# Loading wq whole from one queue instead of in partition halves from two, in a decode-attention kernel

## The chip, the cores and the metric

The kernel runs on one core of one Trainium2 chip. The metric is the device time of one execution in microseconds (us), the median of several runs. Beside it stands one profiled execution, from which all durations come. Its span runs from the first to the last instruction of the program.

## The reference, cut to what matters

One token is decoded: x is one row of 512 values, in bf16.

```
A_x [1,1,512], A_wq [512,4096], A_wo [4096,512], k_cache, v_cache [1,8,65536,128]
q  = layernorm(x) @ wq                       # 32 heads of 128; 4 query heads share one KV head
p  = softmax(q . k / sqrt(128)) over 65536 keys
o  = p @ v                                   # per head
h  = x + o @ wo
h2 = h + (sigmoid(n @ w_gate) * (n @ w_up)) @ w_down,   n = layernorm(h)
```

The K and V caches are 8 heads x 65536 x 128 in bf16 each, together 268 MB; wq is 4 MB. All of it is read once.

## The kernel before, in words

**Data and buffers.** One big SBUF buffer, `ring`, holds 32 chunks of 16 x 128 elements in each of the 128 partitions; `CH` is one chunk (4 KB a partition). The K and V caches of a head come in three loads each, of 12, 8 and 12 chunks (`PIECES`), that is 6, 4 and 6 MB; the helper `load` (lines 318 to 324) issues them. Each load has 128 rows, one for each partition, so a 6 MB load is 128 pieces of 48 KB. wq lies in chunks 24 to 31 of `ring` (32 KB a partition: partition p holds rows 4p to 4p+3 of wq). The third K load of head 0, `K0.2`, goes to chunks 20 to 31, over wq, so it must wait until the q product has read wq.

**Who issues what.** `Prog` keeps one list of operations for each engine, written out by hand in order; `emit` turns them into programs with semaphore waits. All big loads are issued by SyncE (SP) from one queue, q1 in the profile, in this order: wq, K0.0, K0.1, K0.2 (waits for the q product, named `q`), K1.0 (waits for the first 12 chunks of K0 to be transposed, mark `F0.1`), V0.0 (mark `F0.3`), V0.1, K1.1 and so on, two heads interleaved. ScalarE (ACT) issues two small transfers from its own queue, q10.

**The start.** `emit` (lines 195 to 203) takes the first DMA of SP and of ACT out of their lists and puts each into the entry block ahead of the barrier (a Drain) with which every engine starts. The wq load is three DMAs (lines 326 to 328): chunks 0 and 1 of wq (8 KB a partition) for partitions 0 to 63 from SP, the same for partitions 64 to 127 from ACT, and chunks 2 to 7 (24 KB a partition) for all partitions from SP. All three count on one semaphore, `r0`. After the barrier ACT issues x (line 329: `x_col`, 128 pieces of 8 bytes, semaphore `x`).

**From x to K0.2.** VectorE (DVE) copies `x_col` (line 403), makes the layernorm with TensorE (PE, line 388) and GpSimd (POOL, line 399), and writes `xz` (line 406). PE then multiplies `xz` with wq: 32 matmuls in `project_q` (recorded on line 417) and a closing one (line 455). The end of that is `q`. ACT copies the result (line 459), DVE transposes it (line 462), ACT spreads it (line 464), and DVE begins the chunk transposes of K (line 498), 32 for each head in 128x1024 pieces. DVE runs its list in order: the transpose on line 462 stands before the first one on line 498. PE's scores, the softmax and the V product follow, and at the end the output projection and the MLP.

Of the kernel before, what the change touches and what calls it, by code (L numbers as in the profile page):

```python
# [35 lines left out]
class Prog:  # L36
# [14 lines left out]
    def op(self, eng, fn, deps=(), name=None, to=None, times=1):  # L51
        assert name is None or name not in self.where, name
        self.ops[eng].append(dict(fn=fn, deps=[d for d in deps if d], name=name, dma=None, to=to, times=times, part=self.part.get(eng)))
        if name:
            self.where[name] = (eng, len(self.ops[eng]) - 1)

    def dma(self, eng, fn, sem, deps=(), name=None):
        self.op(eng, fn, deps, name)
        rec = self.dma_sems.setdefault(sem, dict(sem=None, count=0))
        rec["count"] += 16  # L60
        self.ops[eng][-1]["dma"] = (sem, rec["count"])

    def emit(self):
# [24 lines left out]
        for e, ops in self.ops.items():  # L88
            n = 0
            for o in ops:  # L90
                if o["dma"]:
                    k, v = o["dma"]
                    value[o["name"]] = (self.dma_sems[k]["sem"], v, k)
                elif o["to"]:
                    k = o["to"]
# [24 lines left out]
        def put(e, eng, o, waits):  # L120
            for sem, v in waits:
                eng.wait_ge(sem, v)
            ins = o["fn"](eng)
            if o["dma"]:
                ins.then_inc(self.dma_sems[o["dma"][0]]["sem"], 16)
            elif o["to"]:
                ins.then_inc(extra[o["to"]], 1)
            elif o.get("inc"):
                ins.then_inc(sems[e], 1)
# [62 lines left out]
            self.nc.switch_bb(end)  # L192

        nc, entry = self.nc, self.nc.cur_bb.bb
        for e, eng, kind in (("sp", nc.sync, mybir.EngineType.SP), ("act", nc.scalar, mybir.EngineType.Activation)):
            first = self.ops[e].pop(0)
            assert first["dma"] and not first["deps"]
            put(e, eng, first, [])
            code = list(entry.instructions)
            load = code.pop()  # L200
            at = [i for i, ins in enumerate(code) if isinstance(ins, mybir.InstDrain) and ins.engine == kind]
            code.insert(at[0], load)
            entry.instructions = code
        entry = nc.cur_bb

        for e, eng in (("sp", nc.sync), ("pool", nc.gpsimd), ("act", nc.scalar), ("dve", nc.vector), ("pe", nc.tensor)):
# [10 lines left out]
def bass_sequential_preLN__gqa_block_cached__glu_gated_glu__decode_kernel(  # L217
# [10 lines left out]
    CH = TC * DH  # L228
    PIECES = ((0, 12), (12, 20), (20, 32))
    RING = 32 * CH  # L230
    AT = {"K": (0, 0, 8), "V": (12, 24, 20), "K0": (0, 12, 20), "V7": (0, 12, 20), "wq": 24, "wg": 0, "wd": 7}
# [7 lines left out]
    with ExitStack() as es:  # L239
        def sb(name, shape, dt):  # L240
            return es.enter_context(nc.sbuf_tensor(name, shape, dt))
# [14 lines left out]
        ring = sb("ring", [128, RING], bf16)  # L256
# [9 lines left out]
        x_col = sb("x_col", [128, 4], bf16)  # L266
# [41 lines left out]
        op, dma = P.op, P.dma  # L308


        W_SPLIT = {"wg": [(0, 4)], "wu": [(0, 3), (3, 4)]}
        W_AT = {"wg": AT["wg"] * CH, "wu": AT["wg"] * CH + 4 * FF}
        LAST = [(20, 28), (28, 32)]
# [9 lines left out]
            at = (first_chunk(k, h, q) - j0) * CH  # L323
            dma("sp", lambda e: e.dma_start(ring[:, at + a * CH:at + z * CH], rows[:, (a - j0) * CH:(z - j0) * CH]), sem, deps, name)  # L324

        for i, (eng, p0, p1, c0, c1) in enumerate((("sp", 0, 64, 0, 2), ("act", 64, 128, 0, 2), ("sp", 0, 128, 2, 8))):
            dst, rows = ring[p0:p1, (AT["wq"] + c0) * CH:(AT["wq"] + c1) * CH], A_wq.rearrange("(p k) n -> p (k n)", p=128)[p0:p1, c0 * CH:c1 * CH]
            dma(eng, lambda e, dst=dst, rows=rows: e.dma_start(dst, rows), "r0", (), "wq" if i == 2 else f"wq{i}")
        dma("act", lambda e: e.dma_start(x_col[:, :], A_x[0].rearrange("o (p k) -> (o p) k", k=4)), "x", name="x")
        for q in range(3):  # L330
            load("K", 0, q, ["q"] if q == 2 else (), f"r{q + 1}", f"K0.{q}")
        for h in range(1, HKV):
# [8 lines left out]
        for i, (j0, nj) in enumerate(WO):  # L341
            src = A_wo[j0 * DH:(j0 + nj) * DH, :].rearrange("(p r) n -> p (r n)", r=nj)
            dst = ktw[:, j0 * D:(j0 + nj) * D]
# [4 lines left out]
        for k, w in (("wg", B_w_gate), ("wu", B_w_up)):  # L348
            src = w.rearrange("(p k) n -> p (k n)", p=128)
            for i, (k0, k1) in enumerate(W_SPLIT[k]):  # L350
                at = W_AT[k]
# [3 lines left out]
        for i, (r0, r1) in enumerate(WD_SPLIT):  # L355
            at = AT["wd"] * CH
# [443 lines left out]
        for i, (nm, bank) in enumerate((("wg", GB), ("wu", UB))):  # L800
            at = W_AT[nm]
            for kt in range(4):
                for c in range(4):
                    dep = [f"{nm}.{j}" for j, (k0, _) in enumerate(W_SPLIT[nm]) if k0 == kt and c == 0]
                    op("pe", lambda e, at=at, kt=kt, c=c, bank=bank: e.matmul(  # L805
# [58 lines left out]
```

## Time and profile before

| | |
|---|---|
| time, median of 3 runs | 660.18 us (660.09 to 660.22) |
| profiled execution, its own time | 660.18 us |
| its span | 658.8 us |
| PE busy | 429.7 us, 65% of the span |
| DVE busy | 350.5 us, 53% |
| ACT busy | 42.9 us, 7% |
| bytes read by DMA | 282.33 MB, 429 GB/s over the span |
| queue q1 (SP) | 8434 packets, 281.81 MB, 99.2% of 16 DMA engines |
| queue q10 (ACT) | 224 packets, 0.53 MB, 0.4% |

The profile gives busy time and idle time of each engine, the chain of waits that ended last, and DMA issues with their time to landing. A DMA is cut into packets, one for each row, that 16 DMA engines move; the trace also holds a record of each packet (start, duration, bytes, queue). "Landing" is when the semaphore of a DMA is complete.

### The profile page before, as it was taken

The numbers are of one execution on the slowest core, as the hardware profiler recorded it, in microseconds if no ns is written. First come the engines' busy times: TensorE is split into PE (matmuls) and PEld (weight loads), VectorE is DVE, ScalarE is ACT, GpSimd is POOL, SyncE is SP. The second block draws the span as 40 slices with busy tenths as digits, with TensorE's granted clock in tenths as the row PEclk, the third lists the DMA queues.
The fourth block names the chain that finished last, engine by engine and source line by source line (L and its number), as shares of the span: only waits on it lengthen the run. The fifth ranks groups of instructions, "written<-read, shape, count | busy, mean of one in ns | idle before, by whom it ended". The sixth has DMA issues, their size and how long they took to land.

```text
span 658.8 us, 6242 instructions
## 1 busy us (share of the span) xinstructions
PE 429.7 (65%) x2315; PEld 69.0 (10%) x1547; DVE 350.5 (53%) x432; ACT 42.9 (7%) x114; POOL 3.6 (1%) x17
## 2 busy tenths in 40 slices
PE   0698576747568467675586476684766855765756
PEld 0100010011001010010000100010100101001212
DVE  2299845838167554647258290684636573573102
ACT  1100200020000200002000200002000020002001
POOL 1000000000000000000000000000000000000000
PEclk9988798777878587796786778785868967778855
DMA  9999999999999999999999999999999999999998
GB/s 350 414 459 433 414 436 424 442 445 419 446 430 430 430 430 462 430 430 430 422 449 436 442 417 430 430 433 442 431 446 430 430 430 430 459 433 410 440 422 336
DMA packets 8658, 282.34 MB, mean 429 GB/s; under 512 B 1105, under 2 KB 1106, under 8 KB 1618
## 3 DMA queue, kind: packets, MB, share of 16 engines
q1 hardware_dynamic: 8434, 281.81, 99.2%
q10 hardware_dynamic: 224, 0.53, 0.4%
HBM read 282.33 MB, written 0.00 MB: 429 GB/s over the span
## 4 chain that ended last, share of the span: by engine, by line
DMA 65%; PE 20%; DVE 11%; issue 3%; ACT 1%; SPq 0%; PEldq 0%; POOL 0%
DMA ring<-in_A_k_cache_dram 34%; DMA ring<-in_A_v_cache_dram 29%; PE PS L417 18%; DVE ktw L498 10%; DMA x_col<-in_A_x_dram 2%; PE PS L805 0%; ACT P_sb L544 0%; DVE M_sb L505 0%; PE PS L823 0%; PE PS L388 0%; PEldq L171 0%; DVE hh L815 0%; SPq L324 0%; SPq L344 0%; PE PS L619 0%
## 5 line engine op out<-in xcount | busy, mean ns | idle before, releaser
L498 DVE STREAM_TRANSPOSE ktw<-ring 128x1024 f32<-128x1024 f32 x256 | 292.5, 1210 | 170.5 <-DMA ring<-in_A_k_cache_dram 170.5
L417 PE MATMUL PS<-ktw 128*128 128x512 bf16 x1024 | 292.4, 437 | 116.6 <-DVE ktw L498 108.3
L417 PE MATMUL PS<-ring,PT_sb 128*32 x1024 | 99.6, 492 | 69.8 <-PEq L171 44.8
L417 PEld LDWEIGHTS PS<-ktw 128*128 x256 | 27.1, 106 | 371.6 <-issue 260.4
L587 ACT ACTIVATE po_sb<-PS,rl 128x512 bf16<-128x512 f32 x8 | 5.5, 687 | 522.7 <-PE PS L417 522.7
L417 PEld LDWEIGHTS PS<-ring,PT_sb 128*32 x1024 | 20.7, 116 | 145.6 <-issue 144.1
L505 DVE TENSOR_REDUCE M_sb<-PS 128x1 f32<-128x512 f32 x32 | 19.9, 684 | 20.5 <-PE PS L417 20.5
L533 DVE TENSOR_REDUCE gmj<-PS 1x4 f32<-1x128 f32 x8 | 2.2, 279 | 39.9 <-PE PS L531 39.9
L544 ACT ACTIVATE P_sb<-PS,negmax 128x512 bf16<-128x512 f32 x32 | 21.6, 686 | 0.3
L554 DVE STREAM_TRANSPOSE PT_sb<-P_sb 128x512 bf16<-128x512 bf16 x32 | 20.1, 682 | 1.7 <-ACT P_sb L544 1.7
L603 DVE TENSOR_TENSOR Lw<-O,blk_of 128x896 bf16<-128x896 bf16 (+1 forms) x2 | 1.4, 682 | 21.8 <-ACT O L593 21.8
L417 PE MATMUL PS<-ring,xz 128*8 x32 | 9.2, 459 | 2.3 <-DVE xz L406 2.3
L388 PE MATMUL PS<-st,onesf 128*128 128x2 f32 x4 | 1.2, 363 | 13.8 <-DVE st L387 13.8
L531 PE MATMUL PS<-identf,gm 128*1 128x128 f32 x16 | 4.5, 379 | 5.6 <-issue 3.4
L538 PE MATMUL PS<-one_f,gmrep 1*128 1x1 f32 x16 | 4.4, 345 | 5.0 <-DVE gmrep L535 5.0
L561 DVE TENSOR_REDUCE lsum<-PS 128x1 f32<-128x4 f32 x8 | 1.3, 162 | 11.8 <-PE PS L559 11.8
L544 ACT ACTIVATION_READ_ACCUMULATOR P_sb<-PS,negmax 128x1 f32 x32 | 6.5, 202 | 0.0
L462 DVE STREAM_TRANSPOSE qt<-qh 32x512 bf16<-32x512 bf16 x1 | 0.7, 699 | 10.7 <-ACT qh L459 10.7
L590 PE MATMUL PS<-sel_bf,po_sb 128*128 128x4 bf16 x32 | 2.1, 170 | 6.3 <-ACT po_sb L587 6.3
L417 PE MATMUL PS<-ktw,O 128*1 x26 | 5.8, 379 | 0.0
L559 PE MATMUL PS<-L_sb,lsel 128*128 128x4 f32 x16 | 2.5, 229 | 3.8 <-DVE PT_sb L554 3.8
L540 ACT ACTIVATE negmax<-PS 128x1 f32<-128x1 f32 x8 | 1.4, 171 | 55.4 <-PE PS L538 55.4
(82 smaller groups left out, 69.1 us busy)
## 6 DMA issues: line engine op xcount, KB each, us to landing
ring<-in_A_k_cache_dram SPq DMA_DIRECT2D x16, 6144.0 KB, 26.1
ring<-in_A_v_cache_dram SPq DMA_DIRECT2D x15, 6144.0 KB, 25.7
ring<-in_A_v_cache_dram SPq DMA_DIRECT2D x9, 4096.0 KB, 30.5
ring<-in_A_k_cache_dram SPq DMA_DIRECT2D x8, 4096.0 KB, 24.7
ktw<-in_A_wo_dram SPq DMA_DIRECT2D x1, 3584.0 KB, 14.7
ring<-in_A_wq_dram SPq DMA_DIRECT2D x1, 3072.0 KB, 13.3
ring<-in_A_v_cache_dram SPq DMA_DIRECT2D x1, 2048.0 KB, 38.4
ring<-in_B_w_gate_dram SPq DMA_DIRECT2D x1, 1792.0 KB, 30.7
```

The costliest lines, as they stand in the source:

```text
L417: return e.add_instruction(mybir.InstMatmult(name=nc.get_next_instruction_name(), engine=mybir.EngineType.PE, ins=[rhs, lhsT], outs=[e.low ...
L498: op("dve", lambda e, d=dst, sr=src: e.transpose(d, sr), deps, f"T{b}.{c}", to="T")
L505: op("dve", lambda e, u=u: e.tensor_reduce(M_sb[:, u % 4:u % 4 + 1], ps(u % NS, 0, 512), AX.X, ALU.max), [f"S{b}.{NC - NR + k}"], f"mx{u}" ...
L531: op("pe", lambda e: e.matmul(ps(MISC, 0, 128, 0, 1), lhsT=gm[:, :], rhs=identf[:, :], start=True, stop=True), [f"gm{h}"], f"gmT{h}", to="Q")
L533: op("dve", lambda e: e.tensor_reduce(gmj[:, :], ps(MISC, 0, 128, 0, 1).rearrange("p (i a c) -> p a i c", a=4, c=NC), AX.XY, ALU.max), [f" ...
L538: op("pe", lambda e: e.matmul(ps(MISC, 128, 129), lhsT=gmrep[0:1, :], rhs=one_f[0:1, 0:1], start=True, stop=True), [f"gmrep{h}"], f"neg{h}")
L540: op("act", lambda e: e.activation(negmax[:, k:k + 1], ps(MISC, 128, 129), AF.Copy, scale=-att_scale), [f"neg{h}"], f"negmax{h}")
L544: op("act", lambda e, b=b: e.activation(P_sb[:, (b % 4) * 512:(b % 4 + 1) * 512], ps(b % NS, 0, 512), AF.Exp, bias=negmax[:, k:k + 1], sca ...
L554: op("dve", lambda e, b=b: e.transpose(PT_sb[:, (b % 4) * 512:(b % 4 + 1) * 512], P_sb[:, (b % 4) * 512:(b % 4 + 1) * 512]), [f"E{b}"], f" ...
L559: op("pe", lambda e: e.matmul(ps(MISC, 132, 136), lhsT=lsel[:, :], rhs=L_sb[:, :], start=True, stop=True), [f"PT{NR * h + NR - 1}"], f"l{h ...
L587: op("act", lambda e: e.activation(po_sb[:, :], ps(PO, 0, 512), AF.Copy, scale=rl[:, :]), [f"PV{h}.{NR - 1}", f"rl{h}"], f"po{h}", to="po")
L590: op("pe", lambda e, t=t: e.matmul(ps(OX, 0, 4), lhsT=po_sb[:, t * 128:(t + 1) * 128], rhs=sel_bf[:, 8 * t:8 * t + 8:2], start=(t == 0), s ...
```

## The change

wq is loaded by one DMA from SP: all 128 partitions, 32 KB each, 4 MB. The two half loads and the 24 KB load are gone. `emit` puts only SP's first DMA ahead of the barrier; ACT's list now begins with x, which is issued after the barrier as before. Semaphore `r0` counts 16 instead of 48. Nothing else differs.

```diff
-        for e, eng, kind in (("sp", nc.sync, mybir.EngineType.SP), ("act", nc.scalar, mybir.EngineType.Activation)):
-            first = self.ops[e].pop(0)
-            assert first["dma"] and not first["deps"]
-            put(e, eng, first, [])
-            code = list(entry.instructions)
-            load = code.pop()
-            at = [i for i, ins in enumerate(code) if isinstance(ins, mybir.InstDrain) and ins.engine == kind]
-            code.insert(at[0], load)
-            entry.instructions = code
+        first = self.ops["sp"].pop(0)
+        assert first["dma"] and not first["deps"]
+        put("sp", nc.sync, first, [])
+        code = list(entry.instructions)
+        load = code.pop()
+        at = [i for i, ins in enumerate(code) if isinstance(ins, mybir.InstDrain) and ins.engine == mybir.EngineType.SP]
+        code.insert(at[0], load)
+        entry.instructions = code
...
+        dma("act", lambda e: e.dma_start(x_col[:, :], A_x[0].rearrange("o (p k) -> (o p) k", k=4)), "x", name="x")
...
-        for i, (eng, p0, p1, c0, c1) in enumerate((("sp", 0, 64, 0, 2), ("act", 64, 128, 0, 2), ("sp", 0, 128, 2, 8))):
-            dst, rows = ring[p0:p1, (AT["wq"] + c0) * CH:(AT["wq"] + c1) * CH], A_wq.rearrange("(p k) n -> p (k n)", p=128)[p0:p1, c0 * CH:c1 * CH]
-            dma(eng, lambda e, dst=dst, rows=rows: e.dma_start(dst, rows), "r0", (), "wq" if i == 2 else f"wq{i}")
-        dma("act", lambda e: e.dma_start(x_col[:, :], A_x[0].rearrange("o (p k) -> (o p) k", k=4)), "x", name="x")
+        dma("sp", lambda e: e.dma_start(ring[:, AT["wq"] * CH:(AT["wq"] + 8) * CH].rearrange("p (k n) -> p k n", k=4),
+                                        A_wq.rearrange("(p k) n -> p k n", p=128)), "r0", (), "wq")
```

## The prediction

> **What bounds the kernel now.** I read the page first, then the DMA issues, the SyncE queue's waits, the timeline and chain of the first 60 us, and last the packet records. The page says that the DMA engines are the bound:
>
> ```profile
> DMA  9999999999999999999999999999999999999998
> GB/s 350 414 459 433 414 436 424 442 445 419 446 430 430 430 430 462 430 430 430 422 449 436 442 417 430 430 433 442 431 446 430 430 430 430 459 433 410 440 422 336
> ...
> q1 hardware_dynamic: 8434, 281.81, 99.2%
> ```
>
> Only the first and the last slice move clearly less. The packet records agree: from 2.2 to 655.5 us at least 14 of 16 DMA engines are always at work, with never a gap on q1. So a microsecond saved in q1's stream at the start comes off the end, and a microsecond in which q1 runs dry is added, whatever PE and DVE do. Two things count: how fast wq passes, and whether the next load is issued before the queue is empty. The edit touches these rows:
>
> ```profile
> ring<-in_A_wq_dram SPq DMA_DIRECT2D x1, 3072.0 KB, 13.3
> ...
> ring<-in_A_wq_dram SPq DMA_DIRECT2D x1, 512.0 KB, 5.4
> ring<-in_A_wq_dram ACTq DMA_DIRECT2D x1, 512.0 KB, 7.5
> ...
> x_col<-in_A_x_dram ACTq DMA_DIRECT2D x1, 1.0 KB, 11.0
> ```
>
> 1 KB of x takes 11.0 us to land, and the chain of waits goes through it:
>
> ```profile
> 1.51 11.04 DMA x_col<-in_A_x_dram
> ...
> 16.09 9.21 PE PS L417 x32
> 25.30 0.23 PE PS L455
> 25.53 0.02 issue
> 25.55 27.90 DMA ring<-in_A_k_cache_dram
> ```
>
> x is read at 12.57, q is ready at 25.55, 12.98 us later, and SyncE then issues K0.2 in that moment. Today this costs nothing, since q1 still holds K0.0 and K0.1: K0.2's first packets come at 37.9 to 38.6 us (mean 38.24), directly behind K0.1's last. Between issue and first packet of a DMA with nothing ahead of it there are 1.37 us (the first wq load, 0.00 to 1.37) or 0.79 us (the output, 657.59 to 658.38); I take 1.1. So q has 38.2 - 1.1 - 25.55 = 11.6 us to spare, and x as much. That is the cover on which the change leans.
>
> **The change, part by part.**
>
> *wq in one load.* The halves run slowly. Alone, an 8 KB packet takes 0.31 us (w_down's, later); the 128 packets of the two halves average 0.54 (SP's) and 0.60 (ACT's): 8 per DMA engine, 2.15 + 2.39 = 4.54 us. The 24 KB packets take 0.912 us each once alone, 0.972 on the mean, since the first overlap ACT's half: 8 per engine, 7.78 us. Together 12.32 us. The windows show the two regimes:
>
> ```profile
> 1.40:6.90 5.50, 0.00 (x0) 0.00 (x0) 2.87 (x9) 1.87 (x2) 2.27 (x11) 1.00 1.06 253
> 7.40:13.70 6.30, 0.52 (x2) 0.50 (x2) 0.52 (x4) 0.00 (x0) 0.00 (x0) 1.00 1.01 433
> ```
>
> The last column is GB/s, 253 against 433. One load of 128 rows of 32 KB is shaped like K0.1, whose packets take 1.213 us without exception: 8 x 1.213 = 9.70. The very first packets of an execution are slow on their own account (0.8 where 0.31 is usual): 0.5 stays. So 12.32 - 10.2 = 2.1 us are gained. The bounds: 2.6 if the first packets aren't slow with full rows, nothing if the slow start is a warm-up that has nothing to do with halves (against it: many second and third packets, at 2.2 to 2.8 us, took 0.31 to 0.45, and the slowness came after). That 128 rows are queued instead of 64 may start some DMA engines later (the 64 rows' first packets spread over 1.4 to 2.2 us): 0 to 0.5. I take 2.1. Two DMAs fewer save 32 semaphore packets of 9 ns over 16 engines, nothing.
>
> *x comes to stand elsewhere in the order.* ACT issues x after the barrier at 1.5 us as before, but now as its first DMA, with wq (9.7 us of work) already in q1 and K0.0 (8 x 1.815 = 14.5 us) issued by SP at the same 1.50. Which goes first? The packet records show how the two queues share an engine:
> - wq0 (SP, 0.00) and wq1 (ACT, 0.12): on all 16 engines the four packets of wq0 and its semaphore come before the first of wq1, without alternation. The two issues ended 85 ns apart.
> - wq2 (SP, 1.504, ending 1.895) and x (ACT, 1.506, ending 1.863): on 15 engines all of x passes first, between 5.63 and 6.92 us. On one, three x packets pass and then one x per wq2 packet, at 7.51, 8.42, 9.34, 10.25, 11.17, and the semaphore at 12.09. That engine alone makes x land at 12.55 and not at 7.4.
>
> So an engine takes packets in the order in which the two queues' DMAs reached it, and mixes them one to one only where both arrive together; 30 ns decide. The first DMA on a queue takes longer to issue:
>
> ```profile
> L328 SPq DMA_DIRECT2D ring<-in_A_wq_dram x2: 391/483/575, 0.0 to 1.5; - x2
> L328 ACTq DMA_DIRECT2D ring<-in_A_wq_dram x1: 539/539/539, 0.1 to 0.1; - x1
> L329 ACTq DMA_DIRECT2D x_col<-in_A_x_dram x1: 357/357/357, 1.5 to 1.5; - x1
> ```
>
> 575 then 391 on SP, 539 then 357 on ACT. As ACT's first, x should take 539: it ends at 2.045. K0.0 as SP's second ends at 1.504 + 0.39 to 0.42 = 1.90 to 1.92. x is 0.13 us behind K0.0 where it was 0.03 ahead of wq2, and 0.3 ahead of K0.1 (from 1.945). It falls behind K0.0 on every engine. K0.0's last packets end at 28.9 - 2.1 = 26.8; x follows within 0.1 and, with the 0.48 us between its last packet and DVE's read today, is read at 27.4 instead of 12.57: 14.8 later. The bounds are 12.5 (x clean ahead of K0.0) and 37 (behind K0.1 too); I take 27.4, by the issue rows.
>
> *The wait that grows.* q then comes at 27.4 + 13.0 = 40.4, and K0.2's first packet at 41.5. K0.1's last ends at 38.2 - 2.1 = 36.1. q1 is dry for 5.4 us. Behind the waiting K0.2 in SP's list stand K1.0 and all others. K1.0 waits for 12 transposes on DVE, which start after line 462, now at 41.0 and done at 41.7 (29.34 before): with the 13.74 us that they take today (29.34 to 43.08) K1.0 is issued at 55.4, first packet 56.5. K0.2 ends 14.6 after 41.5, at 56.1: 0.4 us more. V0.0 waits for 24 transposes, 27.5 us at the same pace: 69.2, while K1.0 keeps q1 busy till 71.1. From there each issue is ahead again. PE and DVE stay under the DMA rate.
>
> Sum: -2.1 + 5.4 + 0.4 = +3.7 us. Profiled execution 660.18 (span 658.8 and 1.4 around it), which is also the median: 663.9 us.
>
> [...]
>
> **The rivals.**
>
> *x gets ahead of K0.0, on the other side.* If the extra 0.18 us of a first issue lies after the moment when the DMA is handed on, or if the engines mix packets from the first, x is through at 12 to 16 us. The price is nothing: q comes by 29, and q1 runs dry only if q is later than 36.1 - 1.1 = 35.0, that is if x is read after 22.0. Then the 2.1 us of wq stand: 658.1 us. For it: 15 of 16 engines before, and the one mixed engine. Against it: the issue durations, and that the worst of 16 engines decides.
>
> *x is mixed into K0.0 part of the way.* One engine like the mixed one today, with six items behind K0.0 packets of 1.815 us, brings x at 11.9 + 11 + 0.5 = 23.4: 1.4 dry, 659.5. More items lead to the forecast. The case in which halves were never the reason for the slow start and x is early also ends near 660. Within 0.2%.
>
> *x falls behind K0.1 too.* Then x is read at 36.8, q at 49.8, K0.2's first packet at 50.9 against 36.1: 14.8 dry, plus 0.4: 673.3. It needs another 0.3 us of delay on ACT.
>
> **How the numbers follow.** Forecast 0.53, x ahead 0.29, mixed or no change 0.08, behind K0.1 0.10. The measurement of this kernel can tell about 0.2% (1.3 us) from no change. Faster 0.29, same 0.08, slower 0.63. The forecast's own range is 661.8 to 666.2: below, 2.6 gained and x up to a packet earlier (1.8 us less dry); above, nothing gained from wq. The range for 8 in 10 must reach the fast case, 657.6 with 2.6 gained, and leaves out the 673 case: 657.6 to 666.4.
>
> **What would show it.** wq in one row of 4096 KB on SP, and K0.0's transposes no longer waiting for a landing but for line 462; packets of 1.2 us from about 2 us on, so K0.0's first packets at 12 and not at 14; x's issue row near 540 ns and its landing at about 25 us; q at 40; a step in the DMA share and GB/s of slices two and three (36 to 41.5 us) and nowhere else. Wrong if x lands before 22 us (then the time is near 658), if the wq packets take more than 1.3 us each, or if q1 shows gaps after 60 us.

## The result and the profile after

The changed kernel takes 657.59 us (median of 6 runs, 657.56 to 658.86) against 660.13 for the kernel before in the same runs: ratio 0.9965, 95% interval 0.9952 to 0.9978. It is faster by about 0.35%. The profiled execution took 657.58 us, its span 656.2. The time went the way of the first rival (658.1), not of the forecast (663.9).

The same lines of the page after the change, DMA share and GB/s in 40 slices, then q1 and the issues:

```profile
DMA  9999999999999999999999999999999999999998
GB/s 400 431 447 431 425 421 431 431 434 436 455 431 431 431 415 434 440 449 425 423 447 431 431 423 444 446 443 431 399 447 431 431 431 431 463 431 411 421 433 348
...
q1 hardware_dynamic: 8354, 282.33, 99.6%
...
ring<-in_A_wq_dram SPq DMA_DIRECT2D x1, 4096.0 KB, 12.2
```

The first slice moved 350 GB/s and now moves 400. No slice shows a hole, and by the packet records at least 14 DMA engines are at work from 1.9 to 653.3 us, but for an instant at 9.25. The chain of waits of the first 60 us (start, length, what) has x at its head again, but what stands behind q is not the same:

```profile
0.81 15.12 DMA x_col<-in_A_x_dram
...
19.48 9.96 PE PS L415 x32
29.44 0.23 PE PS L453
...
30.31 0.70 DVE qt L460
31.01 9.02 DVE ktw L496 x9
```

x is 3.4 us later than before (read at 15.96 instead of 12.57), q 4.1 later (29.67 instead of 25.55), and the K transposes start behind line 460 at 31.01, not at a landing. None of that costs anything: K0.2 is in the queue 6 us before K0.1 runs out. The early windows (last column GB/s) show where the gain is:

```profile
1.40:6.90 5.50, 0.00 (x0) 0.00 (x0) 2.65 (x9) 1.82 (x2) 1.77 (x8) 1.00 0.95 405
```

405 GB/s where the halves moved 253. From the packet records: wq takes 10.28 us per engine instead of 12.32, q1's first packet comes at 1.06 us instead of 1.37, and K0.0's first packets at 11.77 on the mean instead of 14.06. Up to the last load the stream stays 2.24 us ahead (V7.2's packets: 630.17 instead of 632.41). The other 0.4 us of the span come at the end: the engines finish closer together (653.22 to 653.55; before 655.34 to 655.99) and the output's last packet ends 2.20 instead of 2.40 us behind the last of them.

How x came through is plain in the packet records. On each engine three wq packets start first (the earliest at 1.06, 2.86 and 4.07 us); then one x packet passes before each further one:

```
x packets of the 16 engines (us):  5.27-5.78  6.49-7.00  7.70-8.21  9.01-9.43  10.37-10.71  11.58-11.93 (two)  13.41-13.75   semaphore 15.23-15.58
```

Each gap is about one wq packet (1.21 us) or one K0.0 packet (1.82 us). So x overtook wq packets that had been in the queue before it (wq's issue ended at 0.41 us, x's at 1.18), and it did so on all 16 engines.

### The profile page after: what moved, and what is told of

Its sections match the earlier page's. It is cut to its first block, busy times and chain, and to the rows that moved or that the text cites. A ratio compares the mean times of both kernels' runs of the same rounds, so it can differ in the third digit from the quotient of the medians.

```text
span 656.2 us, 6240 instructions
## 1 busy us (share of the span) xinstructions
PE 428.9 (65%) x2315; PEld 69.3 (11%) x1547; DVE 350.2 (53%) x432; ACT 42.9 (7%) x114; POOL 3.6 (1%) x17
## 4 chain that ended last, share of the span: by engine, by line
DMA 61%; DVE 18%; PE 16%; issue 4%; ACT 1%; SPq 0%; PEldq 0%
DMA ring<-in_A_k_cache_dram 30%; DMA ring<-in_A_v_cache_dram 29%; DVE ktw L496 17%; PE PS L415 14%; DMA x_col<-in_A_x_dram 2%; PE PS L803 0%; ACT P_sb L542 0%; DVE M_sb L503 0%; PE PS L821 0%; PE PS L386 0%; PEldq L171 0%; DVE hh L813 0%; SPq L324 0%; SPq L342 0%; PE PS L617 0%
## 5 line engine op out<-in xcount | busy, mean ns | idle before, releaser
L415 PE MATMUL PS<-ktw 128*128 128x512 bf16 x1024 | 288.8, 433 | 116.3 <-DVE ktw L496 104.1
L415 PE MATMUL PS<-ktw,O 128*1 x26 | 7.4, 452 | 0.0
```

The source lines that it names most:

```text
L415: return e.add_instruction(mybir.InstMatmult(name=nc.get_next_instruction_name(), engine=mybir.EngineType.PE, ins=[rhs, lhsT], outs=[e.low ...
```

## Experiments

Theories on x's place: **T**, an engine takes one packet from each queue in turn as soon as both have some, behind the first queue's packets that are already under way; **U**, the prediction's, packets go in the order in which their DMAs arrived. On the halves: **H**, a load into partitions 0 to 63 or 64 to 127 runs at half the rate; **W**, the start is slow anyway; **Q**, the second queue and ACT's DMA ahead of the barrier cost the time. Ratios are to the kernel before, with 95% intervals.

**e1_full_rows_two_queues**, on the kernel before:

```diff
-(("sp", 0, 64, 0, 2), ("act", 64, 128, 0, 2), ("sp", 0, 128, 2, 8))
+(("sp", 0, 128, 0, 1), ("act", 0, 128, 1, 2), ("sp", 0, 128, 2, 8))
```

> The kernel before with its first two wq loads cut by columns instead of partition halves: SP loads chunk 0 (4 KB rows) and ACT chunk 1 (4 KB rows), each for all 128 partitions; both still go ahead of the barrier, x still second on ACT. Theory H (a load into 64 partitions runs at half the rate): the first 1 MB passes in about 16 packets x 0.165 = 2.7 us per engine instead of 4.5, K0.0's first packets come near 12.3 us instead of 14.06, the time is near 658.3. Rival W (the first us of the stream are slow whatever is loaded): no change, 660.1. Rival Q (what cost time were two queues and ACT's DMA ahead of the barrier): 660.1 as well.

658.05 us, 0.9972 [0.9963, 0.9982]; K0.0's first packets at 12.04, on the mean of 16 engines 0.27 us later than in the kernel after. H, within 0.3 us; two queues and ACT's early DMA stayed and cost little. The early window (GB/s last) moved 396 where the halves moved 253:

```profile
1.40:6.90 5.50, 0.00 (x0) 0.00 (x0) 2.76 (x9) 1.87 (x2) 1.89 (x9) 1.00 1.00 396
```

The run also speaks on x's place. x's issue ended 36 ns after that of the third wq load (1.287 and 1.251 us). Under U, where 30 ns decide, all eight of that load's packets would pass first; in the records one passes, and from 5.04 us on x's packets alternate with it one for one. The issue rows (ns, minimum, median, maximum):

```profile
L328 SPq DMA_DIRECT2D ring<-in_A_wq_dram x2: 327/370/412, 0.0 to 0.9; - x2
L328 ACTq DMA_DIRECT2D ring<-in_A_wq_dram x1: 377/377/377, 0.1 to 0.1; - x1
```

The first DMA of each queue takes 412 and 377 here. So the 575 and 539 of the kernel before don't come from being first alone.

**e2_halves_one_queue**, on the kernel after: wq again as two halves and the rest, all from SP.

```diff
+(0, 64, 0, 4), (64, 128, 0, 4), (0, 128, 4, 16)   # partitions, columns of 2 KB; all dma("sp", ...)
```

> The kernel after with wq in the three pieces of the kernel before (two halves of 64 partitions with 8 KB rows, then 24 KB rows), all three issued by SP; x alone on ACT, as in the kernel after. H: the halves run at half rate on one queue too, 1 MB in about 4.5 us, K0.0's first packets near 13.8, 659.6. Q: 657.6, as the kernel after.

1.0007 [0.9998, 1.0017]: as the kernel before, so H and not Q. One more run of the same kernel shows its packets:

> The kernel with the two halves on SP's one queue again, for its packets: 8 KB packets of 0.55 to 0.6 us on the mean, K0.0's first packets near 14 us, 660.

659.92 us; 8 KB packets of 0.575 us on the mean, K0.0's first packets at 13.91. The issues are slow on SP alone too: the first half takes 568 ns, the second 470, but the third load, which covers all 128 partitions, 582:

```profile
L328 SPq DMA_DIRECT2D ring<-in_A_wq_dram x3: 470/568/582, 0.0 to 1.7; - x3
...
1.40:6.90 5.50, 0.00 (x0) 0.00 (x0) 2.87 (x9) 1.87 (x2) 2.18 (x11) 1.00 1.05 250
```

**e7_middle_partitions_first**, on the kernel before:

```diff
-(("sp", 0, 64, 0, 2), ("act", 64, 128, 0, 2), ("sp", 0, 128, 2, 8))
+(("sp", 32, 96, 0, 2), ("act", 0, 32, 0, 2), ("sp", 96, 128, 0, 2), ("sp", 0, 128, 2, 8))
```

> The kernel before with other halves: the first 8 KB a partition go to partitions 32 to 95 (SP, ahead of the barrier), then 0 to 31 (ACT, ahead of the barrier) and 96 to 127 (SP). [...] If any load into 64 partitions is slow: 0.55 to 0.6 us as before, 660.1 or more.

659.16 us in a single run, where the kernel before took 659.73 (659.44 to 660.71) in the same runs; K0.0's first packets at 13.08, against 14.06 in the kernel before and 11.77 in the kernel after. ACT's 32 rows came first, and beside them SP's packets took 0.52 us on the mean (34 until 3.24 us). Once alone, partitions 32 to 95 ran at full speed: 32 packets between 3.24 and 3.95 us with a median of 0.309; the edges that followed (96 to 127) were slow again (the last 30 packets 0.60 on the mean). The windows show it in GB/s (last column):

```profile
1.40:3.20 1.80, 0.00 (x0) 0.00 (x0) 1.47 (x5) 1.35 (x2) 1.80 (x11) 1.00 0.86 228
3.20:4.00 0.80, 0.00 (x0) 0.00 (x0) 0.74 (x4) 0.52 (x1) 0.46 (x1) 1.00 0.99 369
```

So it is not that there are 64 partitions; it matters which. The evidence is thin: 0.7 us of one run. In the kernel before the half 0 to 63 also had a quick stretch (27 packets between 2.2 and 2.85 us, 0.40 on the mean), though there at the start of the load and here after slow packets. And the edit moves the rows of wq in DRAM along with the partitions, so the run does not separate the two. Which of the two it is, and why, was not shown. The halves' packets from 2.85 us on in the kernel before (mean 0.595 us for 8 KB on 16 engines) are 220 GB/s, and those of partitions 32 to 95 at 0.309 us are 424.

**e3_x_behind_K00**, on the kernel after: x is put where the prediction had seen it.

```diff
-        dma("act", ... x_col ..., "x", name="x")       # ahead of all
...
         for q in range(3):
             load("K", 0, q, ["q"] if q == 2 else (), f"r{q + 1}", f"K0.{q}")
+            if q == 0:
+                dma("sp", lambda e: e.dma_start(x_col[:, :], ...), "x", name="x")
```

> The kernel after with x issued by SP between K0.0 and K0.1, so that it passes behind K0.0 on every DMA engine: the place that the prediction gave it. If the prediction's chain of waits is right: x is read at 27.0, q is ready at 40.0, K0.2's first packet comes near 41 while K0.1's last ends at 36.0, 5 us without packets, and with 0.4 for K1.0 the time is near 663.0. Rival (a late q is hidden, K0.2's wait has more cover than I counted): 657.6.

666.26 us, 1.0095 [1.0078, 1.0112]. x is read at 27.15 and q ready at 40.03, as foreseen, and q1 runs dry where foreseen. The chain of waits and two windows (DMA share and GB/s last):

```profile
1.19 25.93 DMA x_col<-in_A_x_dram
...
39.80 0.23 PE PS L454
```

```profile
28.00:35.70 7.70, 5.38 (x16) 1.88 (x17) 0.93 (x5) 0.00 (x0) 0.56 (x1) 1.00 0.95 409
35.80:41.70 5.90, 4.22 (x20) 1.53 (x18) 1.02 (x2) 0.88 (x2) 0.00 (x0) 1.00 0.37 108
```

Against the kernel after, K0.2's packets are 5.99 us later, K1.0's 7.37, K1.1's 7.71, and 7.94 from 184 us on; the span is 8.6 longer. The forecast had 5.4 + 0.4. The dry stretch is 5.3 us over 16 engines; what was left out is the restart: the first 16 packets of K0.2 take 2.61 us on the mean instead of 1.815. The transposes start at 41.38, K1.0 comes 1.4 us late instead of 0.4 and restarts slowly in its turn (its first 16 packets take 2.35). The next loads add 0.6 more. The last 0.7 come at the end, where the engines finish 1.26 us apart (661.03 to 662.29) instead of 0.33.

**e4_x_late_on_ACT**, on the kernel after: x's DMA moved behind ACT's first activation.

```diff
-        dma("act", ... x_col ..., "x", name="x")       # ahead of all
         op("act", ... ["zcol"], "zq")
+        dma("act", ... x_col ..., "x", name="x")
```

> The kernel after with x issued by ACT behind its first activation (line 457 of the kernel before), near 3 us instead of 0.81, when wq, K0.0 and K0.1 have all been in the queue for about 2 us. Theory T (an engine takes one packet from each queue in turn, as soon as both have some, except for the two or three packets that are already under way): x enters about 2 us later than in the kernel after, six packets or so then have to pass among K0.0's, it is read near 20 us, q is ready near 33, nothing runs dry, 657.6. Rival U (packets go in the order in which their DMAs reached the engine, as the prediction had it): x stands behind K0.1, is read near 36.5, 14 us run dry, 671.

657.85 us, 0.9969 [0.9956, 0.9981]. x was issued at 1.77 us (not 3), 0.15 us after SP had finished issuing K0.1. U needed 671. x's packets alternate with wq's from 6.6 us on (5.5 on three engines), and x is read at 17.85:

```profile
1.77 0.37 ACTq L455 DMA_DIRECT2D x_col<-in_A_x_dram  x1
```

```profile
17.85 0.17 DVE L400 CAST hT<-x_col 128x4 f32<-128x4 bf16 x1 [13.68 <-DMA x_col<-in_A_x_dram]
...
31.86 0.70 DVE L460 STREAM_TRANSPOSE qt<-qh 32x512 bf16<-32x512 bf16 x1 [11.06 <-ACT qh L457]
```

T. Another 1.9 us on x, and still nothing on the time.

**e5_small_wq_packets**, on the kernel after: wq in two column halves of 2 MB, in packets of 4 KB.

```diff
+        for i in range(2):   # dst and src "p k n", columns 2048*i to 2048*(i+1)
+            dma("sp", ..., "r0", (), ("wq0", "wq")[i])
```

> The kernel after with wq in two loads by columns (2 MB each, all partitions, 4 packets of 4 KB a row, 32 packets per engine in each), both from SP, the first ahead of the barrier. It asks what the lead is that wq's packets keep over x when x arrives. If it is a number of packets (three, as in the kernel after): x's first packet comes near 2.5 us and all of x is through near 4.5. If it is an amount of data (three packets of 32 KB, so 24 of 4 KB): x's first packet comes near 5 us as in the kernel after, and all of x is through near 7. If packets went strictly in order of arrival (the prediction's reading): x stands behind both wq loads or between them, from 6 us on and in one burst, with nothing alternating. The time is 657.6 in each, plus up to 0.6 for small packets.

658.43 us, 0.9980 [0.9970, 0.9989]. x's first packets come at 4.96 to 5.31 us, behind some 18 packets of 4 KB per engine (289 had started by 5.0), not three; from there they alternate, and all of x is through at 6.74. So what passed ahead of x is no fixed number of packets (18 here, three in the kernel after); in data it is some 72 KB per engine here and 96 in the kernel after. wq's semaphore, not x, is now the last to release q (from the chain of waits):

```profile
1.30 11.54 DMA ring<-in_A_wq_dram
...
13.55 9.69 PE PS L417 x32
```

**e6_x_ahead_of_barrier**, the kernel after with the loop of the kernel before in `emit`, so that x goes out ahead of the barrier:

```diff
+        for e, eng, kind in (("sp", nc.sync, mybir.EngineType.SP), ("act", nc.scalar, mybir.EngineType.Activation)):
```

> The kernel after with x issued by ACT ahead of the barrier, as the kernel before did with its second half of wq. x arrives some 0.7 us earlier and is read 1 us earlier or more. If only the stream of q1 sets the time, the time stays 657.6 whatever x does. If the early start of the barrier was part of the gain (ACT's DMA ahead of it holds the barrier up), up to 0.7 us are lost: 658.3.

657.67 us, 0.9970 [0.9960, 0.9980]. x is issued at 0.12 (its issue ends 0.08 us after wq's), enters after one wq packet and is read at 12.71, 3.25 us earlier than in the kernel after:

```profile
12.71 0.17 DVE L402 CAST hT<-x_col 128x4 f32<-128x4 bf16 x1 [8.43 <-DMA x_col<-in_A_x_dram]
```

The time stays, so x had slack to give and its early landing buys nothing. That one wq packet passes, and not all eight, speaks against U once more.

## Why the prediction was wrong

**x's place: the step that failed.** "So an engine takes packets in the order in which the two queues' DMAs reached it, and mixes them one to one only where both arrive together." The trace of before fits that sentence because its packets were small: wq0, wq1 and x together are 64 KB per engine, and in e5 about that much (72 KB) passed ahead of x. Inside this lead, arrival decided (x before wq2 in the kernel before; x before the second half in e2b, where x's issue ended 76 ns earlier). Behind it, the queues took turns. With 32 KB packets wq itself filled the lead after three (96 KB in the kernel after), and x did not fall behind K0.0 or K0.1 even when it was issued behind both: e4. That turns were taken is shown, by the kernel after, e1, e4, e5 and e6; that the lead explains the bursts is a reading that fits the traces. The lead is no fixed number: 32 KB per engine passed ahead of x in e6, 72 in e5, 96 in the kernel after and 128 on 13 engines in e4. A fixed delay between x's issue and its entry (3.3 to 4.9 us in the last three) would fit those, but e6 (from 2.4) and e2b (from 1.6) speak against it. What the one mixed engine in the trace of before did, all 16 did in the kernel after, and a turn was one record, of 8 bytes or of 32 KB. x's semaphore was complete at 15.93 us, inside the 12 to 16 that were the prediction's estimate for its first rival.

**The issue row.** "The first DMA on a queue takes longer to issue." It was read from two first DMAs that were also the only two half loads. x as ACT's first took 375 ns, about as before (357) and not 539:

```profile
L310 ACTq DMA_DIRECT2D x_col<-in_A_x_dram x1: 375/375/375, 0.8 to 0.8; - x1
```

So even under U, x would have been 38 ns behind K0.0 and not 130. Being first is not the cause (412 and 377 ns in e1). Nor is it half loads alone: loads of all 128 partitions took 582 ns in e2b, and the same K0.1 took 423 in the kernel after, 597 in e1 and 767 in e6. What sets the time of an issue stays open.

**The wait that grows.** It did not arise, since x was read at 15.96 and the bound for that was 22.0. That the chain behind the bound exists e3 shows (x read at 27.15); where the bound itself lies no run tried. The price was too small there (8.6 instead of 5.4 plus 0.4): packets after a dry stretch were priced as running ones, which is 0.7 us of it at K0.2 and part of another 1.0 at K1.0, and the rest, 0.6 over the next loads and 0.7 at the end, had no term.

**wq in one load.** Right in mechanism (e1, e2, e7), small in size: 2.1 forecast, 2.5 measured (2.6 in the profiled executions). The packets gave 2.04. The missing terms are the start of the first packets (0.25 us earlier on the mean of 16 engines; the issue was 0.16 shorter) and the 0.4 us at the end. W is excluded by e1.

**Not foreseen and without effect:** the barrier opens 0.7 us earlier (x is issued at 0.81 instead of 1.51). The last Drain, ACT's behind its half load, took 0.57 us in the kernel before and ended at 1.27; now SP's ends last, at 0.59. DVE, ACT and POOL begin 0.7 us earlier and wait for x all the same.

## What to carry to other kernels

Where one queue keeps the DMA engines full from start to end, price a change at the start by the time at which that queue's next load begins, and separately by whether any later issue can come too late; PE's and DVE's delays in between were worth nothing here until then: x read at 12.71 (e6), 15.96 (the kernel after) and 17.85 us (e4) gave 657.67, 657.59 and 657.85 us, and only at 27.15 (e3) 666.26. Load all 128 partitions at a time: between 1.4 and 6.9 us the halves 0 to 63 and 64 to 127 moved 253 GB/s from two queues and 250 from one (e2b), full rows 396 from two (e1) and 405 from one. Before a row is made into a rule, ask what else sets those two instructions apart, and try the rule on packets of the size that the change will bring.

## What the runs showed of the hardware

- x, 1 KB on a second queue, was not stuck behind the 10 MB (wq and K0.0) on the first in the kernel after, nor behind 14 MB in e4: it entered behind 32 KB per engine in e6, 72 in e5, 96 in the kernel after and 128 on 13 engines in e4, and then took turns packet by packet. Its eight packets per engine and the semaphore came 1.2 to 1.8 us apart in the kernel after (two of them together), so it was complete at 15.93 us; in e5, about 0.18 us apart, all of x was through at 6.74.
- The same DMA took very different times to issue (K0.1: 423 ns in the kernel after, 597 in e1, 767 in e6). A row of one run is no price.
- The queue that ran dry in e3 started slowly: 2.61 us on the mean for K0.2's first 16 packets, which take 1.815 in flow, and 2.35 for K1.0's. So did wq's first packets at the start of the kernel after (1.2 to 2.0 us instead of 1.21).
